# Stores of a memory-augmented attention chain move from the pool and activation queues to the sync queue

## The chip, the cores and the metric

The kernel runs on one core of one Trainium2 chip. The metric is device time in microseconds (us) of one execution. Times of single steps come from one execution that the hardware profiler recorded. TensorE is called PE in the profile, VectorE DVE, ScalarE ACT, GpSimd POOL and SyncE SP; a q behind an engine's name (SPq, ACTq) marks instructions of its sequencer, DMA issues above all.

## The reference, cut to what matters

A sequence of 2048 tokens of width 448 goes through layer norm, then through attention in 64 segments of 32 tokens. Each segment has 8 memory rows in front, and these are the output of the segment before: the chain is sequential. A gated feed-forward layer follows, and the kernel returns the output and the gradients of all inputs and weights.

```python
mem = mem0
for s in range(n_seg):                       # 64 segments of 32 tokens, 8 memory rows
    h = jnp.concatenate([mem, x[:, s*seg_len:(s+1)*seg_len]], axis=1)
    q, k, v = (jnp.einsum('btd,dhe->bhte', h, W) for W in (Wq, Wk, Wv))   # 16 heads of 256
    scores = jnp.where(mask, jnp.einsum('bhqe,bhke->bhqk', q, k) * scale, -1e9)
    o = jnp.einsum('bhqk,bhke->bhqe', softmax(scores), v)
    o = jnp.einsum('bhte,hed->btd', o, Wo)
    mem = o[:, :M]
    outs.append(o[:, M:])
h1 = x + concat(outs)                        # the chain runs on layernorm(x)
out = h1 + (silu(n(h1) @ w_gate) * (n(h1) @ w_up)) @ w_down
# returned: out and, for a given grad_out, the gradients of x, mem0, Wq, Wk, Wv, Wo, w_gate, w_up, w_down
```

## The kernel before, in words

The work has four stages: the forward chain (`forward_chain`, to about 1064 us), the feed-forward phase with its own backward part (`ffn_phase`), the backward chain (`backward_chain`) and a tail of weight gradients (`tail_phase`). The stages are written for Tile: a scheduler orders each engine's instructions by its own simulated times and by priority. What lies inside `with k.prio.crit():` has priority over the rest; the rest fills gaps. `tc.issue_after(ins)` queues the instructions of its block behind `ins` on that engine.

**One segment of the forward chain.** `qk_rows(s, b)` for b = 0, 1 makes the q and k rows of the 32 tokens (lines 521 and 525), and `k.evac` (line 75 on DVE, line 76 on ACT) copies them from PSUM into the staging buffer `qk_st`. `qk_turned(s, b)` transposes them on PE (535) and copies them into `qT` and `kT`. The rows of the 8 memory tokens are added by `rest_rows` on POOL (465) out of `R_b`, which `rest_unit` (454) fills for eight segments at a time. `scores` (603, 609), `softmax` (616 to 623), `value_rows` (633, 641), `transposed_p` (652), `values` (665) and `out_proj` (678) follow. Lines 712 to 722 add the partial results and put the new memory rows, turned, into `hT_roll`, from which the next segment starts; line 722 is the last instruction of a segment's chain.

**What is stored for the backward pass.** Right after `qk_turned(s, 0)` the raw q and k rows are stored from the ACT queue, as `T1q[s]` and `T1k[s]` (line 689, 256 KB each, from the one buffer `qk_st`). At the end of a segment POOL stores the output rows `Oh` (727, 728) and the probabilities `P_all` (729), and SP stores the values `VG` (731, two halves).

**Turned blocks and pieces.** Four segments make a block of 128 tokens (t, with r = 0 to 3 its segment), sixteen make a group (jm = 0 to 15). Attention outputs collect in `xblk` and, for the memory rows, `mblk` (written by POOL, line 739). They are turned by DMA transposes on SP into one of two staging buffers `stg_b` and then stored:

- `to_token_major` (line 543): two halves of `xblk` at r = 3, two halves of `mblk` at jm = 15
- the turned memory rows `T0q` or `T0k` at r = 1 (line 749)
- `piece` (562, 563, 568): one of 44 pieces of the weights, turned, at r < 3 from segment 4 on
- the normalized memory rows `mh` at jm = 15 (line 768)

`stg()` hands out the staging buffers in turn and first issues the store that its buffer still waits for; `save()` keeps the store until then or until `save_all()`, once per segment. All these stores are issued by POOL on line 503, each behind a wait for the transpose's landing.

**Other users of the queues.** `prep_tile` (485, SP, and 488, POOL) brings the rows of a later block into `hT_roll`. `fetch` (585, 586, POOL) and `residual` (576 on DVE, 577 on POOL) add the input to the attention output of a finished block; for a group the fetch waits until the memory product `px` (757, gap-filling matmuls) has been copied to `orow` (758) and stored into `Oh` (759). At the end of the last segment SP loads the feed-forward weights (`k.fl.at(0)` to `at(3)`, lines 282 to 307); the second feed-forward step gets its rows through SP (282, 283) and turned (882) before its matmuls on line 847.

Of the kernel before, what the change touches and what calls it, by code (L numbers as in the profile page):

```python
# [10 lines left out]
BF16 = mybir.dt.bfloat16  # L11
# [4 lines left out]
P = 128  # L16
# [129 lines left out]
def run_all(k: _K):  # L146
    nc, tc, ctx = k.nc, k.tc, k.ctx
    S, D, M, H, Dh, HD, F = k.S, k.D, k.M, k.H, k.Dh, k.HD, k.F
    SEG, L, NSEG, NT, KC, DP, MC, DC, FC = k.SEG, k.L, k.NSEG, k.NT, k.KC, k.DP, k.MC, k.DC, k.FC
# [25 lines left out]
    ident = const.tile([P, P], BF16)  # L175
# [28 lines left out]
    def dt(name, shape, dtype=BF16):  # L204
        return dram.tile(shape, dtype, name=name)
# [3 lines left out]
    dr = dict(XN=dt("XN", [NB * P, DP]), Hh=dt("Hh", [S, D]), HN=dt("HN", [S, D]), DH=dt("DH", [S, D], FP32),  # L209
              DHb=dt("DHb", [NB * P, DP]), Zt=dt("Zt", [S, F]), DGP=dt("DGP", [S, F]), DU=dt("DU", [S, F]),  # L210
              VG=dt("VG", [NSEG, 2 * L, W2]), XR=dt("XR", [NT * 32, DP]), P_all=dt("P_all", [NSEG, P, 8 * L]),
              X_o=dt("X_o", [NB, P, MC * P]), HC=dt("HC", [NB * P, DP]), Oh=dt("Oh", [S, D]))
# [2 lines left out]
        dr["M_" + nm] = dt("M_" + nm, [NT, P, MC * 32])  # L215
    for nm in ("q", "k", "v"):
        dr["T" + nm] = dt("T" + nm, [P, MC, D])
    for nm in ("q", "k"):
        dr["T1" + nm] = dt("T1" + nm, [NSEG, P, 1024])
        dr["T0" + nm] = dt("T0" + nm, [NSEG // 8, P, W2])  # L220
    dr["To"] = dt("To", [P, KC, HD])
    dr["Td"] = dt("Td", [P, KC, F])
# [127 lines left out]
def forward_chain(k: _K):  # L350
    nc, tc = k.nc, k.tc
    S, D, M, H, Dh, HD = k.S, k.D, k.M, k.H, k.Dh, k.HD
    SEG, L, NSEG, NT, KC, DP, MC, DC = k.SEG, k.L, k.NSEG, k.NT, k.KC, k.DP, k.MC, k.DC
    X2 = k.aps["A_x"][0]
    MEM0 = k.aps["A_mem0"][0]
    ident, dr, sel, maskb = k.ident, k.dr, k.sel, k.maskb
    smal = k._small
    W, A, B = k.W, k.A, k.B
# [5 lines left out]
    HB = 4  # L364
    qT_b = [A(2.5 * i, 32, L) for i in range(2)]
    kT_b = [A(5 + 2.5 * i, 32, L) for i in range(2)]
    V_b = [A(11, 2048), W(92, 2048)]
    qk_st = A(15, 2, 2, 512)
    hR_b = [A(19 + 0.5 * i, KC, 64) for i in range(2)]
    R_b = [[W(56 + 4 * i, 32, 64) for i in range(2)], [A(20 + 4 * i, 32, 64) for i in range(2)]]  # L370
    stg_b = [A(36 + 4 * i, 2048) for i in range(2)]
    xblk_b = [A(52 - 24 * i, 32, P) for i in range(2)]
    mblk = A(44, 32, P)
# [4 lines left out]
    or_b = [B(1.25 + 0.5 * i, 32, M) for i in range(3)]  # L378
    x2_t, h_t = B(2.75, D), B(3.625, D)
    hx = B(4.5, KC, P)  # L380
    orow = B(6.25, D)
    P_b = [B(7.125 + 0.625 * i, 8, L) for i in range(2)]
    mh = B(8.375, KC, P)
    om_b = [B(9.375 + 0.5 * i, 256) for i in range(2)]
    maskt = B(10.375, HB * L)

    nc.gpsimd.memset(hT_flat[:, :, NWIN * L:], 0.0)
    nc.gpsimd.memset(PT_bd, 0.0)
    om = k.f32("f1", 256, "om")
    pO = k.po1()  # L390
    nc.vector.memset(pO[:], 0.0)
    nc.vector.tensor_copy(out=maskt.rearrange("p (h n) -> p h n", n=L), in_=maskb[:].unsqueeze(1).to_broadcast([P, HB, L]))
# [122 lines left out]
    def qk_rows(s, b):  # L515
        sl = s % NWIN
        banks = [k.ps1(), k.ps1()]
        for w in range(2):
            for kc in range(KC - 1):
                for q in range(4):  # L520
                    nc.tensor.matmul(banks[w][32 * q:32 * q + 32, :], lhsT=hT_roll[:, kc, sl, M:L], rhs=(Wq_sb, Wk_sb)[w][:, kc, col(q, b)],  # L521
                                     start=(kc == 0), stop=False, skip_group_check=True)
        for q in range(4):
            for w in range(2):
                last = nc.tensor.matmul(banks[w][32 * q:32 * q + 32, :], lhsT=hT_roll[64 * w:64 * w + 64, KC - 1, sl, M:L],
                                        rhs=Wqk3[64 * w:64 * w + 64, col(q, b)], start=False, stop=True, skip_group_check=True)
        for w in range(2):
            k.evac(qk_st[:, w, b, :], banks[w][:], "vs"[w])
        return last

    def qk_turned(s, b):
        pt = k.ps1()[:].bitcast(BF16)
        for w in range(2):
            for i in range(4):
                nc.tensor.transpose(pt[:, w * 512 + i * P:w * 512 + (i + 1) * P], qk_st[:, w, b, i * P:(i + 1) * P], ident[:, :])
        for w, dst in ((0, qT_b[s % 2]), (1, kT_b[s % 2])):
            k.evac(dst[:, 16 * b:16 * b + 16, M:L], pt[:, w * 512:(w + 1) * 512].rearrange("p (c n) -> p c n", n=32), "vs"[w])

    def to_token_major(blk, t, ins=None):
        for hf in range(2):  # L540
            ot = stg()
            with tc.issue_after(ins) if ins is not None else nullcontext():
                nc.sync.dma_start_transpose(out=ot.rearrange("p (a b) -> p a b", b=P),
                                            in_=blk[:, 16 * hf:16 * hf + 16, :].rearrange("p c n -> p (c n)"))
            save((dr["X_o"][t][:, hf * 2048:(hf + 1) * 2048], ot))

    pieces = []
    for nm, Ws in (("d", k.aps["B_w_down"]), ("o", k.Wo2)):
# [39 lines left out]
    for s in range(NSEG):  # L588
        t, r = divmod(s, 4)
        jm = s % 16  # L590
# [7 lines left out]
        with k.prio.crit():  # L598
# [86 lines left out]
                k.fl.at(0)  # L685
                k.fl.at(1)
            qk_turned(s, 0)
            for w, nm in enumerate("qk"):
                nc.scalar.dma_start(out=dr["T1" + nm][s], in_=qk_st[:, w].rearrange("p b n -> p (b n)"))
            value_rows(0)  # L690
            pS0 = scores(0)
            softmax(0, pS0)
# [47 lines left out]
        if due and jm % 3 == 0 and jm > 0:  # L740
            n = due.pop(0)
            residual(n, h_t, x2_t, to_v)
        save_all()
        if (r == 0 and t > 0) or s == 2:
            prep_tile(t + 2)
        if r == 1:
            w = bu // 4
            ot = stg()
            nc.sync.dma_start_transpose(out=ot.rearrange("p (a b) -> p a b", b=P), in_=R_b[bm % 2][w].rearrange("p c n -> p (c n)"))
            save((dr["T0" + "qk"[w]][bm], ot))  # L750
        if r < 3 and s >= 4:
            piece()
        at = None
        if jm == 15:
            px = k.fx1()
# [4 lines left out]
            due = list(range(t - 3, t + 1))  # L760
            if end:
                at = k.fl.at(3).ins
        if r == 3:
            to_token_major(xblk, t, at)
        if jm == 15:
            to_token_major(mblk, NT + s // 16, at)
            mrow = stg()
            nc.sync.dma_start_transpose(out=mrow[:, 0:DP].rearrange("p (a b) -> p a b", b=P),
                                        in_=mh.rearrange("p c n -> p (c n)"))
# [183 lines left out]
def backward_chain(k: _K):  # L953
# [38 lines left out]
    def load_seg(s):  # L992
        if s < NSEG - 1:
            load_v(s)
        for nm, T_sb in (("q", Q_sb), ("k", K_sb)):
            t1 = dr["T1" + nm][s].rearrange("(g x i) n -> g i x n", g=2, x=2)
            t0 = dr["T0" + nm][s // 8].rearrange("(x s i) (g n) -> s g i x n", x=2, s=8, g=2)
            for g in range(2):
                for src, i0, i1 in ((t1[g], M, L), (t0[s % 8, g], 0, M)):
                    nc.sync.dma_start(out=T_sb[64 * g + i0:64 * g + i1].rearrange("p (x c) n -> p x (c n)", x=2), in_=src)  # L1000
        P_sb = Pb[s % 2]
        nc.gpsimd.dma_start(out=P_sb.rearrange("p h n -> p (h n)"), in_=dr["P_all"][s])
        for g in range(2):
            pool_op = nc.gpsimd.tensor_copy(out=P_bd[64 * g:64 * g + L, :, g, :], in_=P_sb[64 * g:64 * g + L, :, :])
        stores("mid", s, pool_op.ins)
# [45 lines left out]
    for s in range(NSEG - 1, -1, -1):  # L1051
        t, r = divmod(s, 4)
        jm = s % 16
# [371 lines left out]
```

## Time and profile before

| | us |
|---|---|
| median of 6 runs | 3192.01 |
| lowest and highest of these | 3181.29, 3206.32 |
| the profiled execution, its own time | 3189.64 |
| its span, first to last instruction | 3187.8 |
| PE busy in it | 2916.3 |
| POOL busy in it | 725.0 |

The mean granted clock of PE is 0.977 of full speed. DMA issues aren't counted as busy time of SP or ACT; POOL's are. The DMA queues of the page: q1 carries SP's transfers, 294.81 MB; q0 POOL's, 220.95 MB; q10 ACT's, 33.56 MB. POOL issues 116 stores on line 503 (40 of X_o with 512 KB each, 16 of T0, 8 of Td, 16 of To, 8 of Tg and Tu together, 24 of Tq, Tk and Tv, 4 of XN). An entry "A <- B" in a list of waits says that A stood until B had ended; the time in brackets in a timeline is the engine's idle time before the instruction.

### The profile page before, as it was taken

To read this page: it belongs to the slowest core of one execution; us is meant where nothing else is said; L and a number is where in the kernel's file an instruction comes from. 1 tells how busy PE (TensorE), PEld (TensorE's weight loads), DVE (VectorE), ACT (ScalarE), POOL (GpSimd) and SP (SyncE) were. 2 spreads that over 40 slices of the span, in tenths; PEclk is the share of its full clock that TensorE was granted. 3 is DMA by queue.
4 is the path that set the end of the run, shared out by engine and by line. 5 is a ranking of instruction groups with operands and counts; after the bars stand their busy time and mean duration, and the time that the engine had idled before them with its cause. 6 is when DMAs were issued, how large, how long until landed. Compare 5 with 4: busy or idle time off the path is not lost.

```text
span 3187.8 us, 107755 instructions
## 1 busy us (share of the span) xinstructions
PE 2916.3 (91%) x47432; PEld 1774.5 (56%) x47442; DVE 1364.4 (43%) x3433; ACT 1057.6 (33%) x2501; POOL 725.0 (23%) x1648
## 2 busy tenths in 40 slices
PE   6899899999988869878999999999999799999998
PEld 3455455555544556655666666666666454444444
DVE  4455455455455467754444444444444200111110
ACT  2444344344444333323333333333333101110210
POOL 2232323323232221121111211112211111121111
PEclk9999999999999989988999999999999899999999
DMA  6967755866667888894444545545645898959952
GB/s 238 200 151 177 196 155 144 197 165 177 166 166 183 253 200 200 201 299 120 132 138 133 142 140 140 130 129 149 136 134 140 262 273 226 200 179 195 187 152 76
DMA packets 757305, 556.21 MB, mean 174 GB/s; under 512 B 627732, under 2 KB 656388, under 8 KB 754404
## 3 DMA queue, kind: packets, MB, share of 16 engines
q1 hardware_dynamic: 671828, 294.81, 43.9%
q0 software_dynamic: 66576, 220.95, 20.5%
q10 hardware_dynamic: 18432, 33.56, 3.0%
q8 instruction: 372, 6.09, 0.8%
q14 instruction: 97, 0.79, 0.1%
HBM read 167.32 MB, written 234.23 MB: 126 GB/s over the span
## 4 chain that ended last, share of the span: by engine, by line
PE 71%; DVE 9%; DMA 7%; issue 7%; ACT 3%; SPq 2%; POOL 1%; ACTq 0%; POOLq 0%; DVEq 0%
PE psf L1286 8%; PE po L1120 7%; PE psf L1071 7%; PE psf L633 5%; PE psf L521 5%; PE psf L1048 4%; PE po L678 4%; PE psf L1307 4%; PE fx L1184 3%; PE psf L847 2%; PE fx L454 2%; DVE arA L75 2%; PE fx L937 2%; PE fx L1291 2%; PE psf L1142 2%
## 5 line engine op out<-in xcount | busy, mean ns | idle before, releaser
L75 DVE CAST arA<-psf 128x256 bf16<-128x256 f32 (+4 forms) x997 | 470.9, 493 | 923.1 <-PE psf L1286 258.9
L76 ACT CAST arA<-psf 128x384 bf16<-128x384 f32 (+6 forms) x979 | 389.9, 420 | 1182.2 <-PE psf L1286 256.5
L1120 PE MATMUL po<-arW,arA 128*32 128x448 bf16 x6144 | 349.4, 357 | 22.4 <-DVE arA L75 19.9
L1286 PE MATMUL psf<-arW,arA 128*128 128x512 bf16 x1000 | 252.0, 379 | 0.0
L633 PE MATMUL psf<-arW,arA 128*64 128x512 bf16 x1536 | 251.3, 391 | 0.0
L1071 PEld LDWEIGHTS <-arW 128*128 128x128 bf16 x8192 | 215.1, 96 | 33.0 <-issue 33.0
L1071 PE MATMUL psf<-arA,arW 128*128 128x40 bf16 x8192 | 219.1, 180 | 13.7 <-issue 8.4
L1286 PEld LDWEIGHTS <-arA 128*128 128x128 bf16 x1440 | 136.0, 98 | 164.8 <-issue 13.7
L1120 PEld LDWEIGHTS <-arA 128*32 128x32 bf16 x6144 | 152.0, 97 | 135.8 <-DVE arA L75 21.1
L521 PE MATMUL psf<-arW,arA 128*32 128x512 bf16 x3072 | 193.8, 385 | 15.4 <-DVE arA L722 12.5
L847 PE MATMUL psf<-arW 128*128 128x256 bf16 x1344 | 156.1, 277 | 43.6 <-DMA arW<-arW 32.0
L847 PEld LDWEIGHTS <-arW 128*128 128x128 bf16 x1344 | 133.4, 99 | 68.9 <-DMA arW<-arW 27.2
L678 PE MATMUL po<-arW,arA 128*32 128x256 bf16 (+1 forms) x4096 | 142.9, 265 | 9.3 <-DVE arA L75 6.8
L1048 PEld LDWEIGHTS <-arW 128*128 128x128 bf16 x2048 | 87.6, 100 | 87.1 <-issue 60.6
L1048 PE MATMUL psf<-arB,arW 128*128 128x80 bf16 x2048 | 98.1, 202 | 39.0 <-DMA arW<-T0k 22.3
L454 PE MATMUL fx<-arA,arW 128*128 128x64 bf16 (+1 forms) x2048 | 84.8, 196 | 43.3 <-ACT arB L76 30.8
L1081 ACT COPY arA<-psf 128x1024 bf16<-128x1024 bf16 x128 | 123.3, 1015 | 2.8 <-PE psf L1080 1.1
L521 PEld LDWEIGHTS <-arA 128*32 128x32 bf16 x3072 | 70.5, 96 | 92.7 <-issue 18.8
L76 ACT COPY arA<-psf 128x512 bf16<-128x512 bf16 (+2 forms) x136 | 78.9, 582 | 106.7 <-DVE arA L75 90.6
L678 PEld LDWEIGHTS <-arA 128*32 128x32 bf16 x4096 | 94.7, 97 | 29.8 <-DVE arA L75 10.2
L633 PEld LDWEIGHTS <-arA 128*64 128x64 bf16 x1536 | 84.6, 110 | 43.5 <-issue 0.9
L454 PEld LDWEIGHTS <-arW 128*128 128x128 bf16 (+1 forms) x2048 | 71.1, 99 | 65.6 <-issue 43.9
(285 smaller groups left out, 4614.2 us busy)
## 6 DMA issues: line engine op xcount, KB each, us to landing
X_o<-arA POOLq DMA_DIRECT2D x40, 512.0 KB, 4.2
T1k<-arA ACTq DMA_DIRECT2D x64, 256.0 KB
T1q<-arA ACTq DMA_DIRECT2D x64, 256.0 KB
arW<-T1q SPq DMA_DIRECT2D x128, 128.0 KB
arW<-T1k SPq DMA_DIRECT2D x128, 128.0 KB
X_v<-arA POOLq DMA_DIRECT2D x32, 512.0 KB, 6.8
X_k<-arA POOLq DMA_DIRECT2D x32, 512.0 KB, 3.8
X_q<-arA POOLq DMA_DIRECT2D x32, 512.0 KB, 3.1
```

What stands on the lines that cost most here:

```text
L75: return nc.vector.tensor_copy(out=out, in_=in_)
L76: return nc.scalar.copy(out=out, in_=in_)
L454: nc.tensor.matmul(banks[w][:, i * 64:(i + 1) * 64], lhsT=lhsT, rhs=xr[lo:hi, kc, :], start=(kc == 0 and i == 0), stop=(kc == KC - 1), ski ...
L521: nc.tensor.matmul(banks[w][32 * q:32 * q + 32, :], lhsT=hT_roll[:, kc, sl, M:L], rhs=(Wq_sb, Wk_sb)[w][:, kc, col(q, b)], start=(kc == 0) ...
L633: nc.tensor.matmul(pV[b][64 * g:64 * g + 64, 0:512], lhsT=hT_flat[:, kc, sl * L:sl * L + 64], rhs=Wv_sb[:, kc, n * 512:(n + 1) * 512], sta ...
L678: nc.tensor.matmul(pO[32 * q:32 * q + 32, 0:w], lhsT=xblk[:, j, r * SEG:(r + 1) * SEG], rhs=Wo_sb[:, cj(j), 256 * dh:256 * dh + w], start= ...
L847: nc.tensor.matmul(ps[:, f2 * 256:(f2 + 1) * 256], lhsT=Wt[:, kc, c * P:(c + 1) * P], rhs=xT[:, kc, :], start=(kc == 0), stop=(kc == KC - 1))
L1048: nc.tensor.matmul(ps[b][:, i * 2 * L:(i + 1) * 2 * L], lhsT=lhs[:, at, :], rhs=rhs_bd[:, cl // 2, :, :].rearrange("p g n -> p (g n)"), st ...
L1071: nc.tensor.matmul(pss[b][:, jj * L:(jj + 1) * L], lhsT=WoT_sb[:, kc, c * P:(c + 1) * P], rhs=do_roll[:, kc, sl, :], start=(kc == 0), stop ...
L1120: nc.tensor.matmul(pH[32 * (j % 4):32 * (j % 4) + 32, 0:D], lhsT=blk[nm][:, j, r * SEG:(r + 1) * SEG], rhs=WT[:, cj(j), :], start=(nm == " ...
L1286: nc.tensor.matmul(pa[2 * kc + g][:, 0:w], lhsT=lhs_of(b)[:, kc * P:(kc + 1) * P], rhs=rhs_of(b, g), start=(b == 0), stop=(b == nblk - 1), ...
L1307: nc.tensor.matmul(pa[i][:, 0:D], lhsT=lhs_of(b, i), rhs=rhs_of(b), start=(bi == 0), stop=(bi == len(nblk) - 1))
```

## The change

Two tensors T1q and T1k become one, T1. Its stores leave the ACT queue and the critical section; SP issues them at the end of the segment, ahead of the value stores. For this there are two staging buffers for each of q and k, used in turn. `save_all` gets the second value store of the segment: the stores it issues then come from SP, behind that one; `stg()` and the last `save_all()` still issue from POOL. The requests for staging buffers are spread anew: the halves of `xblk` of block t − 1 at r = 0 and r = 1 of the next block, T0 at r = 2, pieces at r > 0 except jm = 15, and at jm = 0. To make room, buffers in the arenas change places: `orow` becomes the same memory as `x2_t`, the mask moves from arena B to A, `om` takes the buffer tag f3.

```diff
+    dr["T1"] = dt("T1", [NSEG, P, 2, 1024])
     for nm in ("q", "k"):
-        dr["T1" + nm] = dt("T1" + nm, [NSEG, P, 1024])
...
-    qk_st = A(15, 2, 2, 512)
+    qk_st = [[A(15, 2, 512), A(17, 2, 512)],
+             [k.f32("f1", 512, "q_st")[:].bitcast(BF16).rearrange("p (b n) -> p b n", b=2), B(8.75, 2, 512)]]
...
-    orow = B(6.25, D)
+    orow = x2_t
...
-    om = k.f32("f1", 256, "om")
+    om = k.f32("f3", 256, "om")
...
     def save(*pairs):
-        def fn():
+        def fn(eng=nc.gpsimd):
             for out, in_ in pairs:
-                nc.gpsimd.dma_start(out=out, in_=in_)
+                eng.dma_start(out=out, in_=in_)
         unsaved[rot[0] % 2] = [fn]
 
-    def save_all():
+    def save_all(last=None):
         for i in (1, 2):
             for fn in unsaved.pop((rot[0] + i) % 2, ()):
-                fn()
+                if last is None:
+                    fn()
+                else:
+                    with tc.issue_after(last.ins):
+                        fn(nc.sync)
...
-            k.evac(qk_st[:, w, b, :], banks[w][:], "vs"[w])
+            k.evac(qk_st[s % 2][w][:, b, :], banks[w][:], "vs"[w])
...
-    def to_token_major(blk, t, ins=None):
-        for hf in range(2):
-            ot = stg()
...
+    def to_token_major(blk, t, hf, ins=None):
+        ot = stg()
...
             qk_turned(s, 0)
-            for w, nm in enumerate("qk"):
-                nc.scalar.dma_start(out=dr["T1" + nm][s], in_=qk_st[:, w].rearrange("p b n -> p (b n)"))
...
         nc.gpsimd.dma_start(out=dr["P_all"][s], in_=P_sb.rearrange("p h n -> p (h n)"))
+        for w in range(2):
+            nc.sync.dma_start(out=dr["T1"][s, :, w], in_=qk_st[s % 2][w].rearrange("p b n -> p (b n)"))
         for g in range(2):
-            nc.sync.dma_start(out=dr["VG"][s, L * g:L * g + L], in_=Vs[64 * g:64 * g + L, :])
+            v_out = nc.sync.dma_start(out=dr["VG"][s, L * g:L * g + L], in_=Vs[64 * g:64 * g + L, :])
...
-        save_all()
+        save_all(v_out)
         if (r == 0 and t > 0) or s == 2:
             prep_tile(t + 2)
-        if r == 1:
+        if s >= 4 and ((r > 0 and jm < 15) or (jm == 0)):
+            piece()
+        if r == 2:
             w = bu // 4
             ot = stg()
...
-        if r < 3 and s >= 4:
-            piece()
...
-        if r == 3:
-            to_token_major(xblk, t, at)
         if jm == 15:
-            to_token_major(mblk, NT + s // 16, at)
+            for hf in range(2):
+                to_token_major(mblk, NT + s // 16, hf, at)
             mrow = stg()
...
+        if t > 0 and r < 2:
+            to_token_major(xblk_b[(t - 1) % 2], t - 1, r)
+        if end:
+            for hf in range(2):
+                to_token_major(xblk, t, hf, at)
     save_all()
...
     def load_seg(s):
...
-        for nm, T_sb in (("q", Q_sb), ("k", K_sb)):
-            t1 = dr["T1" + nm][s].rearrange("(g x i) n -> g i x n", g=2, x=2)
+        for w, (nm, T_sb) in enumerate((("q", Q_sb), ("k", K_sb))):
+            t1 = dr["T1"][s, :, w].rearrange("(g x i) n -> g i x n", g=2, x=2)
```

More of the change, by code (lines that the diff above doesn't have):

```diff
@@ L380, in forward_chain @@
     hx = B(4.5, KC, P)
-    orow = B(6.25, D)
[L382 to L385, printed above, removed]
+    orow = x2_t
+    P_b = [B(5.5 + 0.625 * i, 8, L) for i in range(2)]
+    mh = B(6.75, KC, P)
+    om_b = [B(7.75 + 0.5 * i, 256) for i in range(2)]
+    maskt = A(64, HB * L)
     nc.gpsimd.memset(hT_flat[:, :, NWIN * L:], 0.0)
     nc.gpsimd.memset(PT_bd, 0.0)
-    om = k.f32("f1", 256, "om")
+    om = k.f32("f3", 256, "om")
     pO = k.po1()
@@ L534, in qk_turned @@
             for i in range(4):
-                nc.tensor.transpose(pt[:, w * 512 + i * P:w * 512 + (i + 1) * P], qk_st[:, w, b, i * P:(i + 1) * P], ident[:, :])
+                nc.tensor.transpose(pt[:, w * 512 + i * P:w * 512 + (i + 1) * P], qk_st[s % 2][w][:, b, i * P:(i + 1) * P], ident[:, :])
         for w, dst in ((0, qT_b[s % 2]), (1, kT_b[s % 2])):
             k.evac(dst[:, 16 * b:16 * b + 16, M:L], pt[:, w * 512:(w + 1) * 512].rearrange("p (c n) -> p c n", n=32), "vs"[w])
-    def to_token_major(blk, t, ins=None):
-        for hf in range(2):
-            ot = stg()
[L542 to L545, printed above, removed]
+    def to_token_major(blk, t, hf, ins=None):
+        ot = stg()
+        with tc.issue_after(ins) if ins is not None else nullcontext():
+            nc.sync.dma_start_transpose(out=ot.rearrange("p (a b) -> p a b", b=P),
+                                        in_=blk[:, 16 * hf:16 * hf + 16, :].rearrange("p c n -> p (c n)"))
+        save((dr["X_o"][t][:, hf * 2048:(hf + 1) * 2048], ot))
     pieces = []
```

## The prediction

> **What bounds the kernel now.** I read the page's shares and slices first, then the starts of the chain's copy (L722, one per segment) in the timeline, then TensorE's waits in the forward window 50 to 1060 us, then the timelines around each stall and around the hand-over to the feed-forward phase.
>
> ```profile
> PE 2916.3 (91%) x47432; PEld 1774.5 (56%) x47442; DVE 1364.4 (43%) x3433; ACT 1057.6 (33%) x2501; POOL 725.0 (23%) x1648
> ...
> DMA  6967755866667888894444545545645898959952
> ```
>
> TensorE is busy 91% of the span; the change touches only the forward chain, about the first 13 of the 40 slices, and its end. L722 starts at 163.60, 178.69, 193.78: one segment takes 15.09 us, and TensorE's only gap over 0.3 us in it is the 0.78 us of L454, where one filler matmul waits for ACT. Near the block ends a segment takes 16 to 23 us. The waits of TensorE in the forward window that matter here:
>
> ```profile
> PE fx L454 <- ACT arB L76: 30.8, 40, 0.8
> PE psf L609 <- DVE S_sb L617: 16.4, 3, 5.8
> ...
> PE psf L609 <- ACT arA L76: 6.6, 6, 2.5
> ```
>
> L609 are the score matmuls. Columns: us in total, times, longest. So 23.0 us is all that the forward chain loses there; a small change in a stage of a thousand us.
>
> The 6.6 us: in segment 17 ACT comes to the T1 store and stands in front of it until a transpose lands; the copy of turned q and k behind it, which the scores need, starts 3.48 us late.
>
> ```profile
> 324.24 0.33 ACTq L689 DMA_DIRECT2D T1k<-arA  x1
> 324.61 0.58 ACT L76 COPY arA<-psf 128x512 bf16<-128x512 bf16 x1 [3.48 <-DMA arA<-arB]
> ```
>
> The same happens before T1q in segment 5 (3.03 us) and 49 (2.49 us). In all other segments the two issues of 0.33 and 0.40 us lie inside a 0.44 us wait of ACT for DVE and cost nothing.
>
> The 16.4 us are one chain, three times (segments 20, 36, 52): the product of the memory rows (L757) ends late, POOL stores it (L759), the residual's rows are fetched only when that store has landed (L585), and DVE stands at the residual add with the copies for the scores behind it:
>
> ```profile
> 380.99 0.39 DVE L576 TENSOR_TENSOR arB<-arB 128x448 bf16<-128x448 bf16 x1 [5.97 <-DMA arB<-Oh]
> ...
> 383.04 0.46 PE L609 MATMUL psf<-arA 128*40 128x40 bf16 x16 [5.50 <-DVE S_sb L617]
> ```
>
> Last, the hand-over. At 1075 to 1125 us SP works off five transposes of the last segments between the weight loads, and the second feed-forward step gets its rows late:
>
> ```profile
> 1101.32 8.44 SPq L543 DMA_TRANSPOSE arA<-arA  x2
> ...
> 1116.65 2.00 SPq L768 DMA_TRANSPOSE arA<-arB  x1
> 1133.12 11.96 PE L847 MATMUL psf<-arW 128*128 128x256 bf16 x96 [22.67 <-DMA arW<-arW]
> 1050.00:1140.00 90.00, 61.77 (x597) 41.08 (x598) 41.84 (x79) 26.41 (x50) 23.20 (x47) 0.89 1.01 267
> ```
>
> The last line is the window's sums; its end says a DMA share of 1.01 and 267 GB/s. Here the DMA engines are full, elsewhere in the chain they are at 0.64 to 0.83.
>
> **What the skill says.** "DMA: Bandwidth & Descriptors", section "Issuing engines are not separate DMA queues": transfers of all issuers run on the same 16 engines, and another issuer saves only issue time. So the move saves waits in front of issues, not transfer time; this trace has 0.55 us for a POOL issue and 0.33 to 0.40 us for the same kind on ACT. Same page, "SWDGE vs HWDGE vs iDMA": stores from POOL and from SP feed different rings of a DMA engine, which takes turns between them. Same page, "Queues, rings and completion order": within one ring descriptors are consumed in order. So a store moved to SP queues behind SP's earlier loads; the trace agrees at the hand-over, where the first value store behind the weight loads occupies SP for 9.91 us (usually 0.3 to 0.5).
>
> **Part by part.**
>
> 1. *T1 stores, ACT to SP* (128 issues, 0.33 to 0.40 us each). ACT no longer stands in front of them: of the 6.6 us I take 6.0. Bounds: 0 (another wait ends there, such as POOL's own in front of L738, 3.60 us at 324.22) to −6.6. With two staging buffers the next writer is two segments later; a T1 store that is one segment late (15 us) still blocks nobody. **−6.0.**
>
> 2. *Saves of turned blocks and pieces, POOL to SP.* L503 issues 116 DMAs on POOL at 0.53 to 0.66 us. Eight stay: at each third staging request of a block's last segment one is flushed on POOL, three times, and five at the very end. 108 move: about 59 us of POOL issue and most of the 350 us that POOL stands in front of L503. POOL has no time on TensorE's path through them: L609 waits for a POOL copy once, 2.8 us. They matter only through L585. Of L759 and L585 the landings are 5.16+4.34, 3.45+6.19, 5.72+3.46 us, mean 9.4; both run beside two transposes of a block (7.6 us of issue at 366.64). The change spreads those halves over the next two segments, so they are gone there. Calm values: 3.5 for an Oh store, 2.1 to 3.5 for L585 elsewhere; I take 7.0. Against it: the row buffer becomes x2_t, so the fetch of x (L586) now also waits for L759 and takes 0.55 us in front of L585. Gain 9.4 − 7.0 − 0.55 = 1.9 each. **−5.7.** Bounds: +1.7 (only the extra issue) to −16.4 (the add is put further back).
>
> 3. *SP's own load.* Per segment it gets 2 T1 and up to 2 saves, 4 × 0.35 = 1.4 us, to two value stores (0.8) and at most a half block (3.5) and a piece (1.5) or T0 (3.0) and a piece: 7.2 us. The next transpose waits for the save just issued, 4.4 us by POOL's median. 11.6 of 15.09 us: SP keeps up. At a block end three transposes with a POOL save between take some 20 us; the 5 to 8 us of delay are worked off within two segments, and value rows (two buffers) and staging have over 15 us. **0.** Bounds 0 to +5.
>
> 4. *Early segments.* X_o of tile 0 (12.45 us of SP at 110.88) moves to segments 4 and 5. Segment 5 has a 2.81 us gap before L521 without a releaser and one L521 group of 2.75 for 1.48 us; half of 4.1 may go with the traffic. **−2.0**, bounds 0 to −4.1.
>
> 5. *Hand-over.* T0k goes from segment 61 to 62, the last piece beside it, and both saves go on SP behind the last value store, that is behind the weight loads. Now T0k is issued at 1016.86 and all is saved by 1040. So 512 + 448 KB, transposed once and stored once, enter the full window: 1.97 MB at 267 GB/s = 7.4 us, in front of the rows that L847 waits for. **+7.4.** Bounds: +26 (below) to −8 (while SP would wait for the saves the loads for the second step are put ahead; they are now behind two transposes).
>
> 6. Mask, row and softmax buffers change places, om takes another tag, the T1 reads of the backward pass get a row pitch of 4 KB for 2 KB with the same 2 KB runs: **0**, the instructions being the same.
>
> Sum: −6.0 −5.7 −2.0 +7.4 = −6.3 us. The profiled execution took 3189.64 us (span 3187.8), so 3183.3; it is 2.4 us below the median of 3192.01, from which the sum gives 3185.7. I forecast **3184**. A measurement of this kernel tells about 0.5%, 16 us, from no change; the forecast lies inside.
>
> **Rivals.**
>
> *All stalls go.* L609's 23.0 us and the early 4.1 vanish, and the hand-over keeps its length because the step's loads move ahead: 3189.6 − 27 = 3163. For it: POOL has nothing left to wait for, and every stall has a transfer in it. Against: L759 to L585 to L576 is two landings in series, which no queue shortens below some 5 us.
>
> *Slower: one more pass through the two staging buffers at the hand-over.* The segment-62 pair must be turned, landed, saved and landed before the last five transposes can start; and its saves wait in SP's ring behind 5.6 MB of weights. A pass there takes 1101.32 − 1075.27 = 26 us by SP's starts. L847 then waits some 49 us for 22.67. With half of the gains of 1, 2 and 4 the total is +26 − 7 = +19: 3209. It decides if the T0k transpose is issued after the first weight load (L287, now at 1053.71). For it: DMA share 1.01. Against: both inputs are ready before 1050.
>
> *It does nothing:* the T1 stores stand elsewhere, L576 stays, the hand-over absorbs the pair in its waits: 3190.
>
> **Numbers.** Forecast 0.42, all stalls go 0.27, slower 0.25, nothing 0.06. Faster by over 0.5%: 0.27 and a tenth of the forecast, 0.32. Slower: most of the slower rival and the upper end of the forecast, 0.23. Within: 0.45. Both signs being open, the forecast's own range is 3172 to 3196. The whole: low end −6.6 −16.4 −4.1 −8 from 3189.6 is 3154, less a little for run to run scatter (3181 to 3206 in six runs): 3150; upper end +26 +1.7 is 3217, cut to 3211.
>
> **What would show it.** Step 1: no ACT wait with a DMA as releaser in front of the score copies, L609 <- ACT below 1 us. Step 2: the three L609 waits at 3 to 4 us; POOL busy near 665. Step 3: value stores no later than some 10 us after the value casts. Step 5: the 22.67 us of L847 at about 30. It is wrong if the 15.09 us of the plain segment moves (0.2 us are 10 us in all, by another order of fillers), or if qk row casts wait for a T1 store.

## The result and the profile after

| | before | after |
|---|---|---|
| median of all runs, us | 3186.52 (63 runs) | 3185.34 (28 runs) |
| ratio after to before, 95% interval | | 0.9996 [0.9986, 1.0007] |
| span of the profiled execution, us | 3187.8 | 3189.2 |
| POOL busy in it, us | 725.0 | 669.4 |
| first matmul of the last memory product (L757, now L761), us | 1064.05 | 1056.70 |
| first matmul of the second feed-forward step (L847, now L855), us | 1133.12 | 1135.21 |

The change makes no difference that can be measured: 0.0004 of 3186 us is 1.3 us, with an interval of about 3 either way. The forecast of 3184 lies 1.3 us from the median, but with some luck: the median of before over 63 runs is 5.5 us below the six that the forecast started from, and the forecast sum of −6.3 us is a ratio of 0.9980, outside the interval. Below, a line number with a slash is before/after.

The two stage marks in the table say where to look. In these two executions the forward chain ends 7.35 us earlier, and the second feed-forward step starts 2.1 us later: the hand-over between them grew from 69.07 to 78.51 us, by 9.4. Marks of one execution scatter by several us, so the sizes are taken up again below with more executions.

First the page of after, its busy times and its DMA slices:

```profile
PE 2916.2 (91%) x47432; PEld 1760.6 (55%) x47442; DVE 1368.6 (43%) x3433; ACT 1058.5 (33%) x2501; POOL 669.4 (21%) x1540
...
DMA  6767766756755988994445455445545898969941
```

POOL lost the 108 issues (1648 − 1540) and 55.6 us of busy time; no other engine's instructions changed in number. The stores now show up as issues of SP in the page's list (the other 64 of T come from the second pair of staging buffers):

```profile
X_o<-arA SPq DMA_DIRECT2D x33, 512.0 KB
...
T<-arA SPq DMA_DIRECT2D x64, 256.0 KB
```

TensorE's waits from 50 to 1060 us, the answer to the list before (us in total, times, longest):

```profile
PE fx L455 <- ACT arB L76: 19.2, 40, 0.7
PE psf L613 <- ACT arA L76: 16.8, 4, 6.8
PE fx L656 <- DVE arB L627: 16.1, 54, 0.6
```

The first and third line are filler matmuls, which lost 31 us before, nearly all in one place, and lose 35 in two places now; the time of a plain segment hardly changed with it (15.09 to 15.02 us). The score matmuls (L609/L613) lost 23.0 us before and lose 16.8 now. The 5.5 us behind the T1 stores in segments 5, 17 and 49 are gone. The three long waits of segments 20, 36 and 52 are not: 5.69, 6.84 and 3.85 us, 16.4 in sum as before. Only the label went from DVE to ACT. The timeline of segment 20 shows why this is the same stall:

```profile
372.74 0.39 DVE L580 TENSOR_TENSOR arB<-arB 128x448 bf16<-128x448 bf16 x1 [5.98 <-DMA arB<-in_A_x_dram]
...
374.15 0.59 ACT L76 COPY arA<-psf 128x512 bf16<-128x512 bf16 x1 [6.77 <-DVE arA L75]
...
374.79 0.46 PE L613 MATMUL psf<-arA 128*40 128x40 bf16 x16 [5.69 <-ACT arA L76]
```

DVE stands 5.98 us at the residual add (L576/L580), ACT 6.77 us for DVE's copy behind it, TensorE 5.69 us for ACT. What ends DVE's wait has changed: it was the fetch of rows from `Oh`, it is now the fetch of x (L586/L590), in DVE's waits of the same window three times out of three:

```profile
DVE arB L580 <- DMA arB<-in_A_x_dram: 17.2, 3, 7.1
```

The end of the chain and the second step on TensorE:

```profile
1056.70 6.23 PE L761 MATMUL fx<-arW,arA 128*128 128x448 bf16 x32
...
1135.21 13.42 PE L855 MATMUL psf<-arW 128*128 128x256 bf16 x96 [34.12 <-DMA arW<-arW]
```

The wait for the second step's rows went from 22.67 to 34.12 us. In this execution it took all that the chain had won. SP's queue before that:

```profile
1039.72 0.70 SPq L504 DMA_DIRECT2D Tv<-arA  x1
1040.53 1.27 SPq L504 DMA_DIRECT2D X_o<-arA  x1
1044.08 1.47 SPq L572 DMA_TRANSPOSE arA<-in_A_Wv_dram  x1
...
1046.26 0.39 SPq L287 DMA_DIRECT2D arW<-in_B_w_gate_dram  x1
...
1059.37 12.34 SPq L755 DMA_TRANSPOSE arA<-arA  x1
1071.80 0.52 SPq L733 DMA_DIRECT2D T<-q_st  x1
1072.43 0.37 SPq L733 DMA_DIRECT2D T<-arB  x1
1072.90 0.92 SPq L735 DMA_DIRECT2D VG<-arW  x2
1073.86 0.95 SPq L504 DMA_DIRECT2D Tv<-arA  x1
1074.91 1.09 SPq L504 DMA_DIRECT2D T0k<-arA  x1
...
1078.82 13.30 SPq L547 DMA_TRANSPOSE arA<-arA  x2
...
1123.90 5.33 SPq L890 DMA_TRANSPOSE arW<-arW  x2
```

and from the list of SP's waits in 1036 to 1080 us:

```profile
SPq L755 <- DMA arW<-in_B_w_up_dram: 4.6, 1, 4.6
```

The transpose of T0k (L755) starts 13 us after the first weight load (L287). SP first waits 4.6 us until one of these loads has landed, then the transpose occupies it for 12.34 us, where the same instruction took 3.93 us when it was issued before the loads (shown below for another kernel). The two saves at the top, of what was turned in segment 61, free the two staging buffers for the piece (L572) and for T0k. The transposes of the second step's rows (L882/L890) are last in that queue.

### The profile page after: what moved, and what is told of

Its sections match the earlier page's. It is cut to its first block, busy times and chain, and to the rows that moved or that the text cites. A ratio compares the mean times of both kernels' runs of the same rounds, so it can differ in the third digit from the quotient of the medians.

```text
span 3189.2 us, 107909 instructions
## 1 busy us (share of the span) xinstructions
PE 2916.2 (91%) x47432; PEld 1760.6 (55%) x47442; DVE 1368.6 (43%) x3433; ACT 1058.5 (33%) x2501; POOL 669.4 (21%) x1540
## 3 DMA queue, kind: packets, MB, share of 16 engines
q0 software_dynamic: 55168, 175.36, 16.4%
## 4 chain that ended last, share of the span: by engine, by line
PE 72%; DVE 9%; issue 8%; DMA 6%; ACT 3%; SPq 1%; POOL 1%; ACTq 0%; POOLq 0%; DVEq 0%
PE psf L1294 8%; PE po L1128 7%; PE psf L1079 6%; PE psf L526 6%; PE psf L637 5%; PE po L682 4%; PE psf L1056 4%; PE psf L1315 4%; PE fx L1192 3%; PE psf L855 2%; PE fx L455 2%; PE fx L945 2%; DVE arA L75 2%; PE psf L540 2%; PE fx L1299 2%
## 5 line engine op out<-in xcount | busy, mean ns | idle before, releaser
L75 DVE CAST arA<-psf 128x256 bf16<-128x256 f32 (+3 forms) x933 | 426.8, 479 | 821.3 <-PE psf L1294 258.9
L76 ACT CAST arA<-psf 128x96 bf16<-128x96 f32 (+5 forms) x915 | 352.4, 409 | 1079.7 <-PE psf L1294 256.5
L1294 PEld LDWEIGHTS <-arA 128*128 128x128 bf16 x1440 | 135.9, 98 | 164.8 <-issue 13.7
L637 PE MATMUL psf<-arW,arA 128*64 128x512 bf16 x1536 | 220.4, 388 | 0.0
L855 PE MATMUL psf<-arW 128*128 128x256 bf16 x1344 | 158.6, 280 | 52.9 <-DMA arW<-arW 41.4
L855 PEld LDWEIGHTS <-arW 128*128 128x128 bf16 x1344 | 134.8, 100 | 79.1 <-DMA arW<-arW 36.8
L76 ACT CAST arB<-psf 128x64 bf16<-128x64 f32 (+3 forms) x384 | 121.9, 318 | 144.5 <-PE psf L530 108.2
```

Source lines behind the costliest of these rows:

```text
L75: return nc.vector.tensor_copy(out=out, in_=in_)
L76: return nc.scalar.copy(out=out, in_=in_)
L637: nc.tensor.matmul(pV[b][64 * g:64 * g + 64, 0:512], lhsT=hT_flat[:, kc, sl * L:sl * L + 64], rhs=Wv_sb[:, kc, n * 512:(n + 1) * 512], sta ...
L855: nc.tensor.matmul(ps[:, f2 * 256:(f2 + 1) * 256], lhsT=Wt[:, kc, c * P:(c + 1) * P], rhs=xT[:, kc, :], start=(kc == 0), stop=(kc == KC - 1))
L1294: nc.tensor.matmul(pa[2 * kc + g][:, 0:w], lhsT=lhs_of(b)[:, kc * P:(kc + 1) * P], rhs=rhs_of(b, g), start=(b == 0), stop=(b == nblk - 1), ...
```

## The experiments

Two theories were tested. **Mine:** T1's queue gives the gain, the hand-over takes it back, and the wait in segments 20, 36 and 52 is a matter of where the residual add stands. **The rivals:** the stores' move off POOL is what matters (everywhere, or at the chain's end); the transposes of segment 62 cost nothing; or the shared row buffer is to blame for the add. Every ratio is to runs of the kernel before on the same chip. "Mark" stands for the last memory product's first matmul, "hand-over" for the time from it to the second step's; both, like the waits, come from one profiled execution of each kernel.

| kernel | ratio [95%] | mark | hand-over | score waits of segments 20, 36, 52 |
|---|---|---|---|---|
| before | | 1064.05 | 69.07 | 5.50, 5.76, 5.17 |
| after | 0.9996 [0.9986, 1.0007] | 1056.70 | 78.51 | 5.69, 6.84, 3.85 |
| x1, T1 alone on SP | 0.9977 [0.9963, 0.9990] | 1052.80 | 72.40 | 6.34, 9.30, 3.53 |
| x2, after, saves on POOL | 1.0321 [1.0297, 1.0345] | 1164.45 | 73.22 | 7.17, 5.82, 6.58 |
| x3, after, nothing staged in segment 62 | 0.9972 [0.9959, 0.9986] | 1048.22 | 68.70 | 3.45, 3.86, 3.87 |
| x4, after, later add | 0.9943 [0.9920, 0.9965] | 1035.46 | 79.79 | none |
| x5, x3 and x4 | 0.9913 [0.9889, 0.9937] | 1032.62 | 71.38 | none |
| x6, before, later add | 0.9941 [0.9917, 0.9965] | 1051.29 | 68.39 | none |
| x7, after, last saves on POOL | 1.0005 [0.9992, 1.0018] | 1047.96 | 76.90 | 3.42, 4.00, 3.58 |
| x8, after, own row buffer | 1.0005 [0.9988, 1.0021] | 1046.48 | 78.72 | 1.79, 2.86, 3.08 |
| x9, before, T0k and piece in segment 62 | 0.9992 [0.9980, 1.0004] | 1069.49 | 71.17 | 5.87, 5.45, 4.46 |
| x10, x1 and later add | 0.9911 [0.9895, 0.9927] | 1035.67 | 73.37 | none |
| x11, x1 with T1 on ACT | 1.0015 [1.0003, 1.0028] | 1067.35 | 63.92 | 6.26, 5.96, 4.39 |
| x12, after, saves of segment 62 on POOL | 0.9984 [0.9970, 0.9999] | 1051.40 | 73.09 | 7.36, 4.31, 4.54 |

x7 and after have the same forward program up to the last segment, x12 and after up to segment 62. Their marks are 1047.96, 1056.70 and 1051.40 us and the sums of their three waits 11.0, 16.4 and 16.2. A single execution's waits and marks scatter by so much, so below a mark or a wait counts only where several kernels agree. The hand-over is steadier: 76.9 to 79.8 us in after, x4, x7 and x8, which stage the same things at the end of the chain (x7 differs in the last saves alone), and 69.07 and 68.39 in before and x6.

**x1: the T1 part alone.** The two staging buffers and the T1 stores on SP stay; the order of staging and the saves on POOL are those of before.

```diff
-                if last is None:
-                    fn()
-                else:
-                    with tc.issue_after(last.ins):
-                        fn(nc.sync)
+                fn()
...
-        if s >= 4 and ((r > 0 and jm < 15) or (jm == 0)):
-            piece()
-        if r == 2:
+        if r == 1:
...
+        if r < 3 and s >= 4:
+            piece()
...
-        if t > 0 and r < 2:
-            to_token_major(xblk_b[(t - 1) % 2], t - 1, r)
+        if r == 3:
+            to_token_major(xblk, t, at)
```

> T1 stores alone move to SP, with two staging buffers and the changed memory places; saves of turned blocks stay on POOL and the order of staging requests is that of before. Theory (the forward gain comes from the T1 stores, the loss at the hand-over from the pair T0k and last piece that the new order puts into segment 62): the score matmuls wait for no ACT copy behind a T1 store (6.6 us of before gone), the product of the last memory rows starts 5 to 8 us earlier than the 1064.1 us of before, the second feed-forward step waits about 23 us as before, total 5 to 9 us below before, ratio 0.997 to 0.9985. Rival (the saves' move made the forward gain): forward chain as before, ratio 1.000. Rival (T1 stores on SP make the loss at the hand-over): the wait before the second feed-forward step is over 30 us, ratio 1.000 or above.

0.9977 [0.9963, 0.9990], about −7 us: in the total the T1 part is worth what the forecast gave it, and its median ratio is better than that of the whole change. So the other half of the change, saves on SP and the new order, seems to cost some 6 us, though the two intervals overlap a little. Two details were missed: the mark came 11.3 us earlier in place of 5 to 8, and the second step waited 28.00 us in place of about 23, with a hand-over 3.3 us longer than before. The T1 stores are now in SP's queue at the hand-over too.

**x11: x1 with the two issues given back to ACT**, everything else as in x1.

```diff
-            nc.sync.dma_start(out=dr["T1"][s, :, w], ...)
+            nc.scalar.dma_start(out=dr["T1"][s, :, w], ...)
```

> As x1 (two staging buffers, T1 stores outside the critical section at the end of the segment, saves on POOL, old order), but the T1 stores issued by ACT. Theory (it is ACT standing in front of a T1 store until an earlier transfer has landed that costs, so the queue decides): such waits of ACT with a DMA as releaser appear again, 3 us or more in some segments, and the ratio lies at 0.999 to 1.001. Rival (the place in the order and the second buffer decide, not the queue): no such waits, ratio 0.9977 as x1.

1.0015 [1.0003, 1.0028]: the gain is gone. ACT's timeline of x11 in segment 17 has the old stall back, in front of the copy for the scores (those of segments 5 and 49 did not return):

```profile
325.43 0.33 ACTq L733 DMA_DIRECT2D T<-arB  x1
325.80 0.58 ACT L76 COPY arA<-psf 128x512 bf16<-128x512 bf16 x1 [3.19 <-DMA arA<-arB]
```

and its list of TensorE's waits has the old filler wait:

```profile
PE fx L455 <- ACT arB L76: 31.0, 40, 0.8
```

The plain segment is 15.09 us again, where x1 and after have 15.02. So the queue decides, not the second staging buffer. The Trainium skill, "DMA: Bandwidth & Descriptors", section "Issuing engines are not separate DMA queues", says that another issuer saves only the sequencer's time to start a transfer. The runs show more than that: what the sequencer stands behind counts too. The two issues of 0.33 us are a small part of it: segment 17 alone is 20.35 us long in x11 and 16.53 in x1. Nor is this one execution. In the four kernels with the T1 stores on ACT (before, x6, x9, x11) segment 17 takes 20.4 to 23.8 us and segments 3 to 5 together 54.5 to 56.3; in the ten with these stores on SP, 16.5 to 16.7 and 48.6 to 52.8.

**x2: after with every save on POOL**, the new order of staging kept.

```diff
-                    with tc.issue_after(last.ins):
-                        fn(nc.sync)
+                    fn()
```

> The changed kernel, with every save of a turned block issued by POOL again; new order of staging requests and T1 on SP stay. Theory (the pair that is turned in segment 62 fills the hand-over): the wait before the second feed-forward step stays near 30 to 34 us, ratio to before 0.999 to 1.001. Rival (the saves on SP behind the weight loads make the loss): the wait falls to about 23 us and the kernel is 8 to 10 us faster than the changed one, ratio 0.997. On the forward chain: if POOL's saves matter there, its end comes later than 1056.7 us by 3 us or more; theory says within 2 us.

1.0321, about 100 us slower, far beyond what theory or rival had foreseen. With a forward chain so changed, its hand-over (73.22 us, a wait of 28.82) does not decide between them, though it agrees with x12 below. Segments 20, 36 and 52 take 52 to 53 us in place of 21 to 26. Here is POOL in segment 20, then what ACT and TensorE wait for (timelines of x2):

```profile
390.55 0.55 POOL L504 DMA_DIRECT2D Tg<-arA  x1 [5.10 <-DMA arA<-in_B_w_gate_dram]
397.00 0.55 POOL L504 DMA_DIRECT2D Tg<-arA  x1 [5.90 <-DMA arA<-in_B_w_gate_dram]
...
404.89 1.08 POOL L742 COPY arA<-arB 128x256 bf16<-128x256 bf16 x3
```

```profile
405.34 0.33 ACT L76 CAST arB<-psf 128x64 bf16<-128x64 f32 x2 [26.91 <-POOL arA L742]
```

POOL's copies of turned memory rows (L742) stand behind a row of saves, each of which waits about 4 to 6 us for a transpose; ACT needs one of those copies and waits 26.91 us, and TensorE's first matmuls of the next segment wait for ACT. In this order of staging the saves have to be off POOL. In the old order (x1, x10) saves on POOL cost nothing that shows.

**x3: after with nothing staged in segment 62.** T0k is turned in segment 60, the last piece goes into segment 59.

```diff
-        if s >= 4 and ((r > 0 and jm < 15) or (jm == 0)):
+        if s >= 4 and s != NSEG - 2 and ((r > 0 and jm < 15) or (jm == 0)):
             piece()
+            if s == NSEG - 5:
+                piece()
-        if r == 2:
+        if (r == 2 and s < NSEG - 2) or s == NSEG - 4:
```

> The changed kernel with nothing staged in segment 62: T0k is turned in segment 60, the last piece in segment 59 as a second one. Saves stay on SP. Theory: the wait before the second feed-forward step falls from 34.1 to 22 to 26 us and the total by 7 to 10 us against the changed kernel, ratio to before 0.997. Rival (the wait only mirrors the earlier end of the chain: the window is full whatever is in it, so its end is fixed by the weight loads): the second step starts at 1133 to 1136 us as in both kernels, ratio 0.9995.

0.9972 [0.9959, 0.9986], against 0.9996 of after, the two intervals just touching. The hand-over is 68.70 us, 9.8 less than in after and as long as before; the second step's line in TensorE's timeline:

```profile
1116.92 3.38 PE L857 MATMUL psf<-arW 128*128 128x256 bf16 x15 [24.30 <-DMA arW<-arW]
```

So the hand-over grew by what is staged in segment 62, or by how that is queued; x3 takes both away.

**x9: the pair in segment 62, but in the kernel before**, with the saves on POOL.

```diff
-        if r == 1:
+        if (r == 1 and s != NSEG - 3) or s == NSEG - 2:
...
-        if r < 3 and s >= 4:
+        if r < 3 and s >= 4 and s != NSEG - 3:
```

> The kernel before with one thing of the new order: T0k and the last piece are staged in segment 62 instead of 61; all stores stay where they were. Theory (this pair in the full window makes the loss at the hand-over): from the last memory product to the second feed-forward step 73 to 79 us instead of 69.1, total 4 to 10 us above before, ratio 1.0012 to 1.003. Rival (the loss needs the stores in SP's queue): hand-over 67 to 70 us, ratio 1.000.

0.9992 [0.9980, 1.0004], hand-over 71.17 us: against my expectation, the pair alone costs about 2 us. SP's timeline of x9 shows the difference:

```profile
1022.26 3.93 SPq L749 DMA_TRANSPOSE arA<-arA  x1
...
1031.28 1.92 SPq L568 DMA_TRANSPOSE arA<-in_A_Wv_dram  x1
...
1059.15 1.21 SPq L287 DMA_DIRECT2D arW<-in_B_w_gate_dram  x1
```

The scheduler put both transposes 28 to 37 us ahead of the first weight load. In after, the staging buffers of the pair are freed only by the two saves behind segment 62's value store, at 1039.72 and 1040.53 us, and T0k's turn comes after the loads. If that is it, it takes both, the pair late and the saves pinned on SP.

**x12: after with the two saves of segment 62 alone on POOL**, the pair still in segment 62.

```diff
-        save_all(v_out)
+        save_all(None if s == NSEG - 2 else v_out)
```

> The changed kernel with only the two saves of segment 62 (the piece and the half block staged in segment 61) issued by POOL and not behind the value store on SP; T0k and the last piece are still turned in segment 62, the saves of segment 63 stay on SP. In the built order T0k's transpose then stands ahead of the first weight load. Mine, that it takes both (the pair late and the saves that free its buffers pinned on SP): T0k is issued before L287, hand-over 69 to 73 us instead of 78.5, ratio to the kernel before about 0.997. The rival, that the amount of data turned and stored in the full window is what costs, whichever order: hand-over 76 to 79, ratio 0.9990 to 1.0005.

0.9984 [0.9970, 0.9999] and a hand-over of 73.09 us, 5.4 less than in after. In POOL's timeline of x12 the save goes as soon as its transpose has landed; in SP's, T0k is turned ahead of the loads:

```profile
1029.28 0.55 POOL L504 DMA_DIRECT2D X_o<-arA  x1 [5.38 <-DMA arA<-arA]
```

```profile
1032.20 2.79 SPq L755 DMA_TRANSPOSE arA<-arA  x1
...
1040.83 0.38 SPq L287 DMA_DIRECT2D arW<-in_B_w_gate_dram  x1
```

The other save, Tv, went from POOL at 1014.08, and T0k's transpose starts as soon as X_o has landed (1032.18). That is the cause of the larger part of the 9.4 us: two saves on the wrong queue, one segment before the end. x12 also takes T0k's transpose out of the full window, but its 512 KB are only 2 us at the 267 GB/s of before, against the 5.4 gained. A second measure agrees: the time that SP needs from the last large weight load (L304) to the next loads in its queue (L306). It is 11.0 us in before and 21.7 in after; 19.8 to 21.7 in all four kernels whose T0k comes behind the loads (after, x4, x7, x8), 15.5 in x12, 13.5 to 14.8 in the five others with T1 on SP, and 9.3 to 12.3 in the four with T1 on ACT. From L306 to the second step before and after take 58.9 and 59.1 us. So the growth of the hand-over lies in this stretch: some 3 us of it are the T1 stores, the rest T0k and the saves. The ratio alone doesn't part x12 from after (0.9984 to 0.9996, the intervals overlap); the hand-over and the issue order do.

**x7: after with the saves of the last segment alone on POOL**, so that they don't queue behind the weights.

```diff
-        save_all(v_out)
+        save_all(None if end else v_out)
```

> The changed kernel with the saves of the last segment alone (T0k and the last piece) issued by POOL. Theory (the pair's transposes in the full window make the loss, its place in SP's queue included): wait before the second feed-forward step 30 to 35 us, ratio to before 0.998 to 1.001. Rival (its saves behind the weight loads in SP's queue make the loss, since the next transposes must wait for them): wait 22 to 27 us, ratio 0.997.

1.0005 [0.9992, 1.0018], a wait of 32.5 us and a hand-over of 76.90. That rival falls: with the transpose late, the queue of its save changes little.

**x4: after with the residual one segment later.** A segment more between memory product and fetch, and between fetch and add.

```diff
-        if due and jm % 3 == 1:
+        if due and jm % 3 == 2:
...
-        if due and jm % 3 == 0 and jm > 0:
+        if due and jm % 3 == 1 and jm > 1:
```

> The changed kernel, with the fetch and the residual add of each finished block one segment later. Theory (the three waits of the score matmuls, 16.4 us in all, are DVE standing at the add until the fetched rows land): all three waits vanish and the end of the chain comes 14 to 17 us earlier; the total falls by as much if the hand-over moves along, ratio to before about 0.995, or by less than 5 us if the end of the hand-over is fixed by its own transfers. Rival (another wait ends there right after, such as the one for the row copies): the segments 20, 36 and 52 stay at 20 us or more.

0.9943 [0.9920, 0.9965], −18 us. The mark is 21 us earlier than in after and 12 to 16 earlier than in x7 and x12, and DVE doesn't wait at the add (timeline of x4, segment 20):

```profile
378.21 0.17 DVE L724 COPY arA<-psf 128x32 bf16<-128x32 bf16 x1
378.30 0.38 DVE L580 TENSOR_TENSOR arB<-arB 128x448 bf16<-128x448 bf16 x1
```

**x6: the same two lines in the kernel before.**

> The kernel before with nothing but the fetch and the residual add one segment later. Theory (the three waits come from the place of the add on DVE, not from the stores or their queue): the three waits of 5.2 to 5.8 us vanish here too, 14 to 17 us of the chain, hand-over as before near 69 us, ratio 0.9945 to 0.9955. Rival (POOL's saves delay the fetches so much that the add still waits one segment later): waits of 2 us or more stay in segments 20, 36 and 52, or move to 21, 37 and 53, ratio 0.998 or above.

0.9941 [0.9917, 0.9965], all three waits gone: the same gain without any of the change. The stall belongs to the place of the add, on any queue.

**x8: after with a row buffer of its own**, so that the fetch of x needn't wait for the store of the memory product.

```diff
-    orow = x2_t
+    orow = A(10, D)
```

> The changed kernel with a row buffer of its own for the memory product, so that the fetch of x waits for nothing of this group. Theory (the gain forecast for the fetch chain was real for the rows of the attention output, 8.5 us instead of 14.3 us for the three landings of the store, and was eaten by the fetch of x that the shared buffer puts behind that store): the three waits of the score matmuls fall from 16.4 us in all to 8 to 12 us, the total by 4 to 8 us against the changed kernel, ratio 0.9975 to 0.9985. Rival (the add waits for the rows of the attention output alone, whatever x does): waits stay at 15 us or more, ratio 0.9995.

The mechanism shows: x is in time, the adds start with the landing of the `Oh` rows, and the three waits are 7.7 us in place of 16.4. The ratio shows nothing of it: 1.0005 [0.9988, 1.0021]. As x7 has 11.0 us with the shared buffer, the part of the buffer is some 3 to 9 us of wait in a profile, and below what the timing resolved.

**x5 and x10: what the parts give together.** x5 is x3 with x4's lines, x10 is x1 with them.

> The changed kernel with the early pair of x3 and the later add of x4 together. Theory (two separate places, gains add): no waits of the score matmuls over 0.9 us, chain end near 1035 us as in x4, hand-over (last memory product to second feed-forward step) near 69 us as in x3 instead of the 79.8 us of x4; total 26 to 31 us below before, ratio near 0.991. Rival (the full window has a fixed end, an earlier chain end only waits longer): hand-over stays near 80 us, ratio 0.994 as x4.

> T1 stores alone on SP, saves on POOL and old order of staging, as in x1, with the later add of x4. Theory (the saves' move is not needed; what helps is T1 off ACT and the later add): chain end 1034 to 1040 us, hand-over 69 to 73 us, total 24 to 29 us below before, ratio 0.991 to 0.9925, the same as x5. Rival (with the add out of the way POOL's saves are next): chain end above 1042 us with waits of the score matmuls behind POOL, ratio 0.994.

0.9913 [0.9889, 0.9937] and 0.9911 [0.9895, 0.9927], medians of 3160.7 and 3158.6 us: some 28 us below before, and not to be told apart. x10 leaves all saves on POOL and the old order of staging. Of the change only the T1 part is needed for the fastest kernel of this study.

## Why the prediction came out

**Step 1, T1 off ACT, −6.0: held for the stalls it names, with more beside them.** The waits of the scores behind T1 fell by 5.5 us; x11 brings back the one in segment 17, 2.2 us. But "in all other segments the issues cost nothing" was wrong: the plain segment went from 15.09 to 15.02 us, a movement of the kind that the prediction had named as a sign of error. It makes between 2 and 3 us over some forty segments; 2.0 of them are given back in segments 56 to 62, which went from 103.2 to 105.3 us in sum. Beside that, segments 3 to 5 are some 5 us shorter with T1 on SP (means of ten kernels against four), and the T1 stores cost some 3 us at the hand-over. That x1 as a whole gained about 7 us, close to the 6.0, is in part luck.

**Step 2, the fetch chain, −5.7: failed in size.** Its "9.4 to 7.0" was right: the three landings of store and rows took 28.3 us in sum before, 21.1 in after and 19.1 to 20.2 in x3, x7 and x12, which have the same program there. The mis-sized term was "0.55 us" for the fetch of x behind the shared buffer. It is a whole fetch that comes onto the path, not an issue: x, which had landed long before in the old kernel, now lands 3.9 and 2.4 us after the rows in segments 20 and 36 of after, and once took 7.95 us. One landing was shortened, another put behind it. The three waits stayed at 16.4 us in after and 16.2 in x12; they fell to 11.0 and 11.2 in x7 and x3, where x lands at most 2.1 us after the rows. The mean of the four is a gain of 2.7 us for 5.7. x8 fits: with its own buffer the landings are 19.4 us in sum and the waits 7.7. x4 and x6 show the lever that the step only named as a bound.

**Step 3, SP's own load, 0: held.** No cast of qk rows waits for a T1 store and no value store is late up to segment 61. x2 adds what the step lacked: in this order of staging, POOL is no alternative.

**Step 4, early segments, −2.0: the size came out, for another reason.** Segments 1 to 5 take 88.9 us before and 87.3 after: segment 5 wins 6.3 us, segments 3 and 4 lose 4.2. The step gave this to the store of tile 0 that moves to later segments. But x1 and x10 keep the old order and take 84.6 and 87.5 us; x11, with the same order and T1 on ACT, takes 90.6. So the gain goes with T1's queue.

**Step 5, hand-over, +7.4: the sign held, the size was +9.4, the mechanism only in part.** The wait of L855 is 34.1 us for "about 30". The step priced the added bytes; x12 shows that the larger part is SP standing in its queue. The slower rival's deciding point was met as well, T0k behind L287, yet it cost no 26 us, and the cause lay one segment further ahead than the rival put it: not the pair's own saves (x7) but those that free its buffers (x12). Its price counted a whole pass of SP's queue, but in before SP already stood in the full queue for 9.91 us, at a value store. In after it waits 4.6 us and stands for 12.34 at the transpose, and the two value stores take 0.92 us: part of the stand moved, and from L304 to L306 10.7 us were added. The trace fits the Trainium skill, "DMA: Bandwidth & Descriptors", section "Queues, rings and completion order", which has the descriptors of a ring consumed in order: T0k's transpose takes 12.34 us behind the loads for 3.93 ahead of them.

**Step 6 and the rest, 0: held.** From the second feed-forward step's start to the end, after takes 0.7 us less of span than before.

In sum, for the two profiled executions: −7.35 us up to the chain's end (−13.7 forecast), +9.4 at the hand-over (+7.4 forecast), −0.7 later, +1.4 us of span. The first of these is poorly known. The marks are 1064.05 and 1069.49 in before and x9, which has the same program up to segment 60, and 1047.96 to 1056.70 in after, x3, x7 and x12: every pair has the chain end earlier, by 7 to 22 us. Part of that is the choice of executions: after's profiled one took 5.9 us more than the kernel's median, x7's 11.8 less. So the chain's gain may well be as large as forecast; that it fell short by step 2 is shown by the waits, not by the marks. The total's −1.2 ± 3.4 us, from the ratio, is the better number, and it says that gain and loss cancel. The rival "all stalls go" failed in the same step 2. "It does nothing" has the right total for a wrong reason, since the chain does end earlier.

**Open.** From the second step's start to the end a single execution took 2045.3 to 2060.0 us in before, x6 and x9, which don't differ there; this too is why marks alone prove little. x8's missing gain in the total isn't explained. Why segments 3 to 5 are shorter with T1 on SP was not traced, nor the rest of the 4 us by which x12's hand-over is still longer than before's.

## What to carry to other kernels

Ask of a store which engine's queue it stands in and what stands behind it there: taken from the engine whose next copy is on the path, it gives back its stall and not only its issue time. Pinning a store behind another on a queue also holds every later user of its buffer to that queue's order; where the queue is about to be filled by a bulk load, free the buffers first. And when two transfers in series end a wait, look for a later place for the one who waits before shortening a transfer.

## What the runs showed of the hardware

A DMA transpose on SP of 512 KB (T0k) took 3.98, 3.93 and 2.79 us of issue ahead of the weight loads (before, x9, x12), and 12.34 us in after behind some 6 MB of them (the prediction's 5.6 MB counts their large parts alone), besides 4.6 us of wait in front of it. SP issued nothing else in that time. Waits of POOL of 4 to 7 us for the landing of a transpose cost nothing that shows where they were spread over the segments (before, x1, x10); in x2 four of them in a row, 3.8 to 5.9 us each, in front of one small copy were most of a 26.91 us wait of ACT.
